# One written order of issue for the whole kernel, with batch 0's attention in two query ranges and the first range as token group 0

## The chip, the cores and the metric

The kernel runs on one core of a Trainium2 chip. Times are device microseconds (us) of that core. "Timed" means the median of plain executions; "span" means the length of the one execution that the profiler recorded, which is 1.7 to 1.9 us shorter than the time of the same execution.

The engines are TensorE (PE in the profile, PEld for its weight loads), VectorE (DVE), ScalarE (ACT), GpSimd (POOL) and SyncE (SP).

## The reference

Squared-ReLU attention, followed by a feed-forward layer with a quick GELU (called the expert layer below).

```python
q, k, v: (8, 12, 448, 64)        # batch, heads, sequence, head_dim
scores = q @ k.T / sqrt(64)
attn   = maximum(scores, 0)**2 / 448
x      = (attn @ v)              # -> 3584 tokens x 768
h      = x @ w_in                # 768 x 2048
g      = h * sigmoid(1.702 * h)
out    = g @ w_out               # 2048 x 768
```

## The kernel before

Attention works on units: 4 of the 12 heads of one batch, so 3 units a batch and 24 in all. Unit u has seven score slots `s u.0` to `s u.6`, one for every 64 keys. A slot is four concurrent 64x64 groups of matmuls, a ReLU from PSUM (on ScalarE, or on VectorE where the slot is marked `d`) and a square on VectorE (`x u.j`). When all seven squares of a unit are there, `a u` multiplies with v and evacuates the result into `xt`, the input of the expert layer.

```python
def relu2(u, j, sc, dve=False):
    ...
    if dve:
        nc.vector.tensor_scalar(out=rl, in0=sc[:, :, 0:S], scalar1=0.0, scalar2=None, op0=ALU.max)
    else:
        nc.scalar.activation(out=rl, in_=sc[:, :, 0:S], func=AF.Relu)
    ...                                   # square now, or when the list says x u.j
```

The expert layer works on groups of tokens, counted in blocks of 64 (`gblk`). First product of step f of group g: six matmuls into `ht`, the gate on ScalarE (`gf`), a scaling on GpSimd (`gt`). The second product of group 0 is plain (32 matmuls for 128 tokens); the later groups use pairs that share sums of weights (56 matmuls for 256 tokens), with a single of 32 where 128 tokens are left over. The sums of weights need all four loaded parts of w_out.

```python
gblk = [6, 8] * (B // 2)                  # 384 and 512 tokens by turns
...
def cast(u, n, eng): ...                  # float32 load -> float16, k on ScalarE, q on GpSimd
def trans(u):   nc.sync.dma_start_transpose(...)       # kT, qT through the DMA
def w2(h, i):   nc.gpsimd.dma_start(out=wout[h][i], in_=...)   # casting load of part i, half h
```

The order of issue is the order in which the program is written; no scheduler moves anything. Up to about 110 us it is a list of words (below, cut). After that a rule mixes first and second products in proportion and puts in a "visit" (three score slots, sometimes an attention product) for every 4.8 us of expert work.

```python
words = ("z3 s0.0 s0.1 x0.0 x0.1 q1 z3 s0.2 ... f14 f15 Q6 K6 R6 x5.5 ... m2 m1 F0 B2 W6 ...").split()
...
for it, tv in moe:                        # the rule, from group 2 on
    ...
    while acc >= tv and visits:
        step_visit()                      # prefetches loads, casts and transposes too
```

## Time and profile before

| | kernel before |
|---|---|
| timed, median of the first 3 runs | 393.91 us (392.98 to 394.2) |
| span of the profiled execution | 391.4 us, granted clock 0.997 |
| first matmul of the expert layer | 31.0 us |
| first matmul of its second group | 64.6 us |
| after the last matmul | 5.4 us |

This is the view of waits of TensorE in the kernel before, from 110 to 330 us; the columns are who waited for whom, us in total, how often, and the longest.

```profile
PE ht L294 <- ACT gf L299: 1.3, 4, 0.3
PE op L361 <- DVE osb L372: 0.5, 1, 0.5
PE op L361 <- ACT ea L370: 0.4, 1, 0.4
PE sc L145 <- ACT rl L159: 0.4, 1, 0.4
```

These named waits add up to 2.6 us. The distances between matmul starts show 7.5 us lost in the same stretch, in the form of small delays that never make the engine idle for long. So the whole document uses one measure, "lost time": the distance from one matmul's start to the next, less its undisturbed distance (columns / 2.4 GHz + 2.5 ns; a quarter of that for each of four concurrent 64x64 matmuls, half for the transposes), less 0.1 us for each change among the three shapes that matmuls have here (the full array, the transposes' 128x64 and the 64x64 tiles; 132 changes before, 135 after).

### The profile page before, as it was taken

How to read it: one execution, taken by the hardware profiler on the slowest of the kernel's cores; microseconds unless marked ns; L12 is line 12 of the kernel's file. 1: busy time of each engine (PE TensorE's matmuls, PEld its weight loads, DVE VectorE, ACT ScalarE, POOL GpSimd, SP SyncE). 2: the span in 40 equal slices, each digit the busy share in tenths (PEclk: the TensorE clock that was granted, in tenths of full speed). 3: DMA queues.
4: the chain of work that ended last, by engine and by line, in shares of the span. 5: the costliest groups of instructions: out<-in, count | busy, mean ns of one | idle time of the engine just before them, and what ended most of it. 6: DMA issues, size and time to landing. Idle time of an engine off the chain costs nothing.

```text
span 391.4 us, 7859 instructions
## 1 busy us (share of the span) xinstructions
PE 375.0 (96%) x3134; PEld 193.6 (49%) x3134; DVE 247.3 (63%) x408; ACT 226.1 (58%) x329; POOL 138.6 (35%) x200
## 2 busy tenths in 40 slices
PE   8779999999999999999999999999999999999993
PEld 3444455445455555444455555444454555554552
DVE  1898965898767675557566767265676767113473
ACT  2887672766676664776675656767675662242210
POOL 8545343634543333242443322341342221232100
PEclk9999999999999999999999999999999999999998
DMA  8999999998956808762474909673234301110323
GB/s 117 195 203 205 204 283 197 197 228 169 197 110 163 203 6 242 145 146 81 77 209 126 226 20 204 122 196 97 52 92 33 82 2 40 42 41 0 83 80 81
DMA packets 65221, 50.85 MB, mean 130 GB/s; under 512 B 35744, under 2 KB 61728, under 8 KB 65184
## 3 DMA queue, kind: packets, MB, share of 16 engines
q1 hardware_dynamic: 47872, 35.70, 36.2%
q0 software_dynamic: 17152, 14.55, 25.4%
q8 instruction: 24, 0.39, 0.4%
q10 hardware_dynamic: 160, 0.10, 0.1%
q14 instruction: 13, 0.11, 0.1%
HBM read 45.61 MB, written 11.01 MB: 145 GB/s over the span
## 4 chain that ended last, share of the span: by engine, by line
PE 78%; DVE 9%; ACT 7%; issue 4%; DMA 1%; POOL 0%; ACTq 0%; POOLq 0%
PE ht L294 32%; PE op L361 26%; PE sc L145 8%; PE av L185 7%; ACT rl L159 4%; PE op L322 4%; DVE osb L372 3%; DVE at L590 3%; ACT k L102 1%; ACT gf L299 1%; DMA q<-in_q_dram 1%; PE tr L129 1%; DVE at L173 1%; PE sc L594 1%; DVE xt L205 0%
## 5 line engine op out<-in xcount | busy, mean ns | idle before, releaser
L159 ACT ACTIVATE rl<-sc 128x896 f16<-128x896 f32 x159 | 140.5, 922 | 39.7 <-PE sc L145 39.4
L294 PE MATMUL ht<-xt,win 128*128 128x384 f16 (+1 forms) x768 | 160.8, 353 | 1.8 <-ACT gf L299 1.3
L301 POOL TENSOR_SCALAR gt<-gf 128x384 f16<-128x384 f32 (+1 forms) x128 | 84.9, 663 | 212.7 <-ACT gf L299 211.6
L299 ACT ACTIVATE gf<-ht 128x384 f32<-128x384 f32 (+1 forms) x128 | 70.1, 548 | 93.9 <-PE ht L294 83.6
L294 PEld LDWEIGHTS <-win 128*128 128x128 f16 x768 | 71.9, 98 | 76.8 <-issue 15.8
L173 DVE TENSOR_TENSOR at<-rl 128x896 f16<-128x896 f16 x105 | 67.8, 672 | 16.4 <-ACT rl L159 16.4
L361 PEld LDWEIGHTS <-gt 128*128 128x128 f16 x408 | 39.0, 98 | 32.1 <-issue 6.0
L145 PE MATMUL sc<-qT,kT 64*64 64x448 f16 x696 | 50.0, 361 | 2.8 <-ACT rl L159 1.8
L590 DVE TENSOR_TENSOR at<-rl 128x896 f16<-128x896 f16 x63 | 41.6, 683 | 8.1 <-ACT rl L159 7.9
L361 PEld LDWEIGHTS <-as 128*128 128x128 f16 x312 | 30.0, 98 | 23.7 <-issue 3.9
L372 DVE SCALAR_TENSOR_TENSOR osb<-op,osb 128x384 f32<-128x384 f32 (+1 forms) x45 | 23.6, 545 | 28.2 <-PE op L361 28.0
L361 PE MATMUL op<-wsum,gt 128*128 128x384 f16 x224 | 40.7, 326 | 0.5 <-ACT ea L370 0.4
L361 PE MATMUL op<-wout,as 128*128 128x384 f16 x224 | 40.7, 326 | 0.3
L205 DVE CAST xt<-av 128x896 f16<-128x896 f32 (+2 forms) x34 | 25.8, 784 | 19.0 <-PE av L185 18.9
L185 PE MATMUL av<-at,v 64*64 64x448 f16 x644 | 34.8, 350 | 0.5 <-ACT rl L159 0.2
L361 PE MATMUL op<-wout,gt 128*128 128x384 f16 (+1 forms) x184 | 32.4, 319 | 1.6 <-DVE osb L372 0.9
L145 PEld LDWEIGHTS <-kT 64*64 64x64 f16 x696 | 17.9, 105 | 29.5 <-issue 20.9
L372 DVE SCALAR_TENSOR_TENSOR osb<-op,ea 128x384 f32<-128x384 f32 x22 | 12.1, 552 | 25.9 <-PE op L361 14.6
L185 PEld LDWEIGHTS <-v 64*64 64x64 f16 x672 | 20.1, 107 | 13.3 <-issue 3.5
L356 DVE TENSOR_TENSOR as<-gt 128x1024 f16<-128x1024 f16 x36 | 26.3, 756 | 0.0
L91 POOL DMA_DIRECT2D v<-in_v_dram x24 | 18.0, 750 | 5.5 <-DMA win<-in_moe_w_in_dram 2.4
L104 POOL CAST q<-qst 128x896 f16<-128x896 f32 x18 | 17.9, 993 | 1.0
(39 smaller groups left out, 178.0 us busy)
## 6 DMA issues: line engine op xcount, KB each, us to landing
out_dram<-osb SPq DMA_DIRECT2D x54, 192.0 KB, 3.1
kst<-in_k_dram SPq DMA_DIRECT2D x18, 448.0 KB, 4.5
qst<-in_q_dram SPq DMA_DIRECT2D x18, 448.0 KB, 5.1
v<-in_v_dram POOLq DMA_DIRECT2D x24, 224.0 KB, 4.4
win<-in_moe_w_in_dram POOLq DMA_DIRECT2D x8, 384.0 KB, 11.5
wout<-in_moe_w_out_dram POOLq DMA_DIRECT2D x4, 768.0 KB, 12.1
k<-in_k_dram POOLq DMA_DIRECT2D x6, 224.0 KB, 9.3
q<-in_q_dram POOLq DMA_DIRECT2D x6, 224.0 KB, 9.3
```

Of the source, the lines that this page charges most:

```text
L145: nc.tensor.matmul(out=sc[c, a, 0:S], lhsT=st["kT"][r, j, c], rhs=st["qT"][r, :, c], start=True, stop=True)
L159: nc.scalar.activation(out=rl, in_=sc[:, :, 0:S], func=AF.Relu)
L173: nc.vector.tensor_tensor(out=at, in0=rl, in1=rl, op=ALU.mult)
L185: nc.tensor.matmul(out=st["av"][s][64 * a:64 * a + 64, 0:S], lhsT=st["v16"][r, a, 64 * j:64 * j + 64], rhs=at[r, a, :], start=(j == 0), st ...
L205: nc.vector.tensor_copy(out=xts[g][:, 2 * pr:2 * pr + 2, c], in_=st["pair"][:, :, f])
L294: nc.tensor.matmul(out=ht[:, 0:n], lhsT=w[:, kk, fo:fo + 128], rhs=xts[g][:, kk, 0:n], start=(kk == 0), stop=(kk == NK - 1))
L299: nc.scalar.activation(out=gf[:, 0:n], in_=ht[:, 0:n], func=AF.Gelu_apprx_sigmoid, scale=1.0 / SC)
L301: nc.gpsimd.tensor_scalar(out=gts[g][:, f, 0:n], in0=gf[:, 0:n], scalar1=SC, scalar2=1.0, op0=ALU.mult, op1=ALU.mult)
L356: nc.vector.tensor_tensor(out=out_, in0=x, in1=y, op=op)
L361: nc.tensor.matmul(out=op[:, 0:cw], lhsT=lhs[:, f, :], rhs=w[:, f, c0:c0 + cw], start=(start and f == 0), stop=(stop and f == HF - 1))
L372: nc.vector.scalar_tensor_tensor(out=o, in0=op[:, 0:w], scalar=sc, in1=add, op0=ALU.mult, op1=ALU.add)
L590: nc.vector.tensor_tensor(out=at, in0=rl, in1=rl, op=ALU.mult)
```

## The change

The intent: start the expert layer earlier, by making its first group out of the first 256 queries of batch 0, and let one optimised list decide every instruction's place instead of the rule. The groups become 4, 8, 8, 8, 6, 8, 6, 8 blocks. The diff, cut to its core:

```diff
-    gblk = [6, 8] * (B // 2)
+    gblk = [4, 8, 8, 8, 6, 8, 6, 8]
...
+    QA = gblk[0]
+    split = slots_of(0, QA) + slots_of(QA, J - QA)     # 4 slots for 256 queries, 3 for 192
+    whole = [[(j, 0, J, 0)] for j in range(J)]
+    def pieces(u):
+        return split if u < NP else whole
...
-        for s in [0, 1] * times:
-            for a in range(2):
+        for kb, q0, q1, c0 in pieces(u)[j] * times:
+            for s in range(2):
+                for a in range(2):
...
+              "a": lambda how, u: av(how, u, 0, J if u >= NP else QA),
+              "b": lambda how, u: av(how, u, QA, J),
...
-        for it, tv in moe:          # the rule, with mix(), visits and prefetch(): all removed
...
+        words = (
+            "z3 jq0 jk0 I jk1 q0 jq2 k0 s0.0:d x0.0 ... s1.6 jk5 x1.5 x1.6 s2.4 jw1 f0.0 ...
+            ... f0.14 s5.0 f0.15 x4.6 Q6 x5.0 ... m0.1.0 a5 m0.0.0 f1.0 jo1.1 jo1.0 f1.1 f1.2
+            Q7 R6 f1.3 s6.0 L8 ... f1.15 s9.0 x8.5 R10 x8.6 L11 a8 W10 s9.1 s9.2 p1.0.0 ...
+            ... p7.2.5 p7.2.6").split()
```

The words: `b u` is the attention product of unit u's second query range, `f g.f` step f of group g's first product, `m`, `p`, `i` are plain, pair and single steps of the second product, `jo h.i` the load of w_out's half h, part i, `A` to `E` its sums, `L`/`W` the loads of q and k / of v, `K` and `Q` the casts, `R` the transposes, `:d` a ReLU on VectorE.

## The prediction

> **What bounds the kernel now.** I read the page's busy shares first, then busy time by stretch, then the chain of work that ended last in two stretches, then VectorE's timeline at the start.
>
> The page's first part (busy time, share of the span, instructions):
>
> ```profile
> PE 375.0 (96%) x3134; PEld 193.6 (49%) x3134; DVE 247.3 (63%) x408; ACT 226.1 (58%) x329; POOL 138.6 (35%) x200
> ```
>
> TensorE (PE) is the only engine near full, so the time is its work plus its gaps. To see where the gaps are, busy time in chosen stretches; columns are the stretch, its length and the busy time and instruction count of PE, weight loads, VectorE, ScalarE and GpSimd, then granted clock, DMA share and rate:
>
> ```profile
> 0.00:31.00 31.00, 24.78 (x341) 12.18 (x341) 20.42 (x39) 19.94 (x24) 19.07 (x32) 1.00 1.11 173
> 31.00:65.00 34.00, 33.39 (x337) 17.23 (x334) 23.86 (x36) 21.13 (x32) 13.57 (x21) 1.00 1.22 227
> 65.00:110.00 45.00, 45.00 (x362) 21.53 (x361) 38.67 (x61) 30.03 (x43) 22.37 (x29) 1.00 1.00 200
> 110.00:330.00 220.00, 216.40 (x1791) 112.35 (x1790) 140.35 (x231) 142.00 (x208) 73.01 (x102) 1.00 0.50 115
> 330.00:386.00 56.00, 55.41 (x314) 30.29 (x312) 23.62 (x44) 12.99 (x23) 10.61 (x17) 1.00 0.19 49
> 386.00:391.40 5.40, 0.01 (x1) 0.00 (x0) 0.36 (x1) 0.00 (x0) 0.00 (x0) 0.75 0.52 139
> ```
>
> Three things: PE loses over 6 us before 31 us, where the first matmul of the expert layer (`ht`) stands; nothing from 65 to 110; 3.6 us from 110 to 330, in bits. The border at 110 is one in the source: up to there the order of issue is a written list, after it a rule spreads the visits. The chain says the same, first for 60 to 110 us, then for 110 to 330 us:
>
> ```profile
> by line: PE ht L294 47.7%; PE op L322 31.0%; PE sc L145 11.3%; PE av L185 7.9%; PE op L361 2.6%
> ```
>
> ```profile
> by line: PE op L361 34.6%; PE ht L294 30.5%; PE av L185 9.1%; PE sc L145 8.7%; ACT rl L159 4.4%; issue 3.7%; DVE osb L372 3.2%; ACT k L102 2.2%; ACT gf L299 1.3%; DVE at L173 1.2%; DVE as L356 0.6%; DVE osb L448 0.3%; ACT eb L370 0.2%; ACT
> ```
>
> In the listed stretch the chain never leaves PE; in the ruled stretch 17% of it runs through ScalarE, VectorE and issue. Busy time hides part of this, since matmuls overlap: I compared the distance between successive matmul starts with their undisturbed distance (162 ns for 384 columns, 215 ns for 512) and find 7.5 us lost from 110 to 330 us, 0.3 us from 60 to 110, 10.7 us before 30 us.
>
> What holds the start? VectorE's timeline (start, length, engine, line, operation, count, idle before):
>
> ```profile
> 10.14 0.62 DVE L590 TENSOR_TENSOR at<-rl 128x896 f16<-128x896 f16 x1 [2.25 <-ACT rl L159]
> ...
> 12.20 0.62 DVE L133 COPY kT<-tr 128x896 f16<-128x896 f16 x1
> ...
> 14.02 2.28 DVE L590 TENSOR_TENSOR at<-rl 128x896 f16<-128x896 f16 x4
> 16.76 1.28 DVE L208 CAST xt<-avm 128x384 f16<-128x384 f32 x4 [0.47 <-PE avm L185]
> ```
>
> From 10 us on VectorE has hardly a gap: squares, copies of transposed tiles, evacuations. It is busy 18 of 20 us between 10 and 30, ScalarE beside it 17.6. So the first 31 us are bound by preparing attention, not by PE.
>
> **What the Trainium skill says.** "Trainium Kernel Development and Optimization", Performance Expectations, calls matmul busy time a bad measure because matmuls are pipelined. The trace agrees: 3.6 us idle against 7.5 us lost. "TensorE: Matmul & The Clock Gate", section "Wait — 56ns, not 53.3ns?", gives N ÷ 2.4 GHz + about 2.5 ns from start to start for a warm array, 215.8 ns for 512 columns; the chain's late row of twelve `ht` matmuls in 2.59 us makes 216, so I trust it for 256 columns (109 ns). The same section puts a floor of about 25 ns under every matmul however short; nothing in this trace is short enough to show it. "TensorEngine Tiling (Array Packing)", Key Properties, says that changing the tiling mode drains the engine: eight `op` matmuls take 1.30 us in the chain after other full ones and 1.41 after attention's 64x64 ones, so about 0.1 us a switch is seen.
>
> **The change part by part.**
>
> *PE's work.* Groups 4,8,8,8,6,8,6,8 put 2 row blocks of 128 in the group that uses the plain second product (32 matmuls a block) where it was 3; 8-groups use pairs (56 for two blocks), 6-groups a pair and a single (88 for three). Before 96 + 3·88 + 4·112 = 808; after 64 + 5·112 + 2·88 = 800. Eight fewer at 0.1625 us is -1.3 us. The six doubled score slots (marked t, pure filler) go: each is four concurrent matmuls, 0.189 us (28 of `av` take 1.32 us), so -1.1 us. Mode switches go from 132 to 135 in the built order: +0.3. First-product columns are unchanged.
>
> *Short matmuls.* Batch 0's three units are cut into 19 pieces where there were 7 slots, for scores and again for `av`, of 64 to 256 columns. The columns are the same. With a floor of 25 ns per matmul a group of four costs at least 100 ns: against 27 ns of columns at 64, 53 at 128, 80 at 192, 107 at 256. The order has 12, 12, 21 and 12 such groups of scores, as many of `av`: at most 2·(12·69 + 12·43 + 21·16) = 3.4 us, an estimate from that page. At least it is some 0.2 us, and part lies in time when PE waits anyway: I take +1.0.
>
> *The start.* The first `ht` no longer waits for all 21 slots of batch 0, but for 12 (its first 256 queries). In VectorE's order 13 squares, 6 copies, a relu and six 128x256 evacuations stand before it: nominally 16 us with the rows' durations (square 0.60 back to back, copy 0.62, relu 1.08, evacuation 0.42 between the 0.21 and 0.55 of 64 and 384 columns), where before it was 22. Before, 22 us were done in 31.1 - 6.2, 89%. The same rate puts the first `ht` at 24.5 us. But that is not yet the gain, as the second group needs all of batches 0 and 1, the same 42 slots as before. Up to its first matmul VectorE has 42·0.60 + 5·1.08 + 12·0.62 + 8.1 (evacuations) + 0.6 = 47 us, before 46. At 89 to 95% it comes to 55.5 to 59 us; PE has 43.5 - 11 = 32.5 us of work between its first `ht` and there, so without a gap 24.5 + 32.5 = 57, which I take; before it was 64.6. By then less PE work is done: 43.5 us counted against 50 (10.5 of first product instead of 15.6, no doubled slots). So the start loses 57 - 43.5 = 13.5 us where it lost 14.6 to 14.7. That is only -1.2. It rests on the 89%; at 95% it is -2.7. Since an optimised list should pack VectorE better, and ScalarE has 39 us of work by then and is not in the way, I take -2.3.
>
> *The rest as a list.* The written stretch from 60 to 110 us lost 0.3 us with VectorE busy 38.67 of 45; the ruled one lost 7.5. If the new list is as good, it saves up to 7. It carries more on VectorE, however: 20 relus there instead of 9 (11·1.08 = 12 us), two more pair sets. Between the middle of group 1's first product and group 2's, VectorE's count is 25 us beside 26 of PE, and in the stretch where one group's second pair stands in a row it is 16 beside 15. I take half to two thirds of the 7.5 as saved: -4.8.
>
> *The end.* The last 14 pair steps are the same in both, so the 5.4 us after the last matmul stay.
>
> Sum on PE's path: 391.4 - 1.3 - 1.1 + 0.3 + 1.0 - 2.3 - 4.8 = 383.2. The median of timed runs is 2.5 over the profiled span (393.9 against 391.4), so 385.7.
>
> **Rivals.** First, VectorE becomes the bound of the middle: for it, the counts just given and 18 us more in total (20 relus); against it, the old listed stretch ran gapless at 86%. Then the rule's 7.5 us stay in another place and the time is 389 to 392. Second, the short matmuls cost their full 3.4 us, and on VectorE's chain: 388. Third, weights come late: the DMA moves some 200 GB/s from 10 to 50 us and is at its limit there; first-group first products want `win` part 1 at about 34 us and part 3 at 45. At 200 GB/s the list's order lands them near 27 and 37 us, so I expect no wait; if one comes, each late part is 2 to 4 us. Fourth, everything pays: the second group at 55 us and 1 us of gaps in the rest makes 381.
>
> **Range and chances.** The terms that I can't fix are the start (-5 to +1), the gaps (-7 to 0) and the short matmuls (+0.2 to +3.4). They are independent, about ±4.5 us together: 381 to 390.5. Two per cent faster is 386.0, within half a microsecond of my number, so faster gets 0.52, same 0.45, slower 0.03.
>
> **What would show it.** Right: first `ht` near 24.5 us, first of the second group at 55 to 59; the chain from 110 to 330 almost all PE; 800 `op` matmuls of 384 columns, counting two of 192 as one; four-matmul groups of 64 columns starting 30 to 100 ns apart. Wrong: PE idle before `op` or `ht` with VectorE named as releaser through the middle; `ht` waiting on a `win` transfer; the second group's start over 60 us; a last stretch other than 5.4 us.

## The result

| | before | after |
|---|---|---|
| timed, median of 4 runs each | 393.98 (392.98 to 394.2) | 389.69 (389.49 to 390.16) |
| span | 391.4 | 388.4 |
| granted clock | 0.997 | 0.999 |

A ratio is the mean time of one kernel's fast runs over that of the other's in the same rounds, so it isn't quite the ratio of the medians. Here it is 0.9898 (95%: 0.9879 to 0.9917): 1.0% faster, within the 2% that counts as the same, where 2.1% faster was predicted. The time lies inside the range of 381 to 390.5, near its upper end.

The page's first part for the kernel after (busy time, share of the span, instructions):

```profile
PE 370.6 (95%) x3390; PEld 195.4 (50%) x3390; DVE 262.4 (68%) x433; ACT 218.4 (56%) x320; POOL 136.8 (35%) x200
```

VectorE has 15 us more, ScalarE 8 us less, mainly because 11 more ReLUs (20 for 9) run on VectorE. TensorE's count grows by the short matmuls. The same stretches as in the prediction, in the same columns (stretch, length, busy time and count of PE, PEld, DVE, ACT, POOL, then clock, DMA share, GB/s; the DMA share is the sum of the packets' times over that of the 16 DMA engines, and as these times overlap it can pass 1):

```profile
0.00:31.00 31.00, 24.16 (x591) 15.90 (x595) 21.27 (x41) 20.87 (x28) 17.82 (x32) 1.00 1.10 172
31.00:65.00 34.00, 32.84 (x400) 18.91 (x393) 24.78 (x43) 22.29 (x36) 16.57 (x26) 1.00 1.12 215
65.00:110.00 45.00, 41.49 (x342) 18.72 (x341) 37.62 (x56) 32.14 (x46) 22.39 (x27) 1.00 1.07 216
110.00:330.00 220.00, 219.40 (x1778) 113.06 (x1776) 156.20 (x254) 130.56 (x191) 69.99 (x101) 1.00 0.53 114
330.00:383.00 53.00, 52.40 (x297) 28.71 (x296) 22.22 (x42) 12.49 (x22) 10.06 (x16) 1.00 0.19 50
383.00:388.40 5.40, 0.33 (x4) 0.10 (x2) 0.36 (x1) 0.00 (x0) 0.00 (x0) 0.93 0.55 147
```

Read the third and the fourth line against those of before. From 110 to 330 us PE's idle time falls from 3.60 to 0.60 us, as hoped. From 65 to 110 us, where the kernel before had none at all (45.00 of 45.00), there are now 3.51 us. The change gives back in one stretch what it gains in another.

The chain of waits from 60 to 110 us of the kernel after: first the shares by line, then the start, length and kind of three of its pieces.

```profile
by line: DMA wout<-in_moe_w_out_dram 27.3%; PE ht L245 18.8%; PE op L271 11.0%; DVE at L453 10.8%; PE sc L166 7.0%; PE op L310 6.6%; DVE rl L177 4.2%; PE av L197 3.7%; ACT gf L250 2.4%; issue 2.3%; DVE xt L217 2.1%; POOL wout L411 1.9%; ACT
...
60.80 0.94 POOL wout L411
...
61.75 13.66 DMA wout<-in_moe_w_out_dram
...
75.45 2.77 PE op L271 x16
```

In the kernel before, this chain was all PE. Here it leaves PE for over half of the stretch. It runs through the load of the second half of w_out, which the list issues at 60.8 and 61.7 us; the kernel before issued its two parts at 44.2 and 53.0 us. The view of waits has PE standing for it once:

```profile
PE op L271 <- DMA wout<-in_moe_w_out_dram: 2.4, 1, 2.4
```

The second place is the row `DVE at`, 10.8% of the chain. The timeline of the kernel after (start, length, engine, line, operation, output and input, count, idle before and its releaser) shows the square that does it, and what PE does afterwards:

```profile
89.02 1.08 DVE L177 TENSOR_SCALAR rl<-sc 128x896 f16<-128x896 f32 x1
...
89.69 0.77 POOL L91 DMA_DIRECT2D v<-in_v_dram  x1
...
90.02 1.88 DVE L453 TENSOR_TENSOR at<-rl 128x896 f16<-128x896 f16 x1
...
90.47 0.94 POOL L104 CAST q<-qst 128x896 f16<-128x896 f32 x1
...
95.97 1.45 PE L197 MATMUL av<-at,v 64*64 64x448 f16 x24 [0.52 <-DVE rl L177]
97.99 0.38 PE L197 MATMUL av<-at,v 64*64 64x448 f16 x4 [0.57 <-DVE at L453]
```

A square of this shape takes 0.62 us; this one takes 1.88, beside GpSimd's issue of the load of v and its cast of q for unit 10. It ends 0.49 us after the cast does. VectorE's queue is 1.3 us late from then on, and PE pays in the next attention product, 5 us later: lost time of 1.45 us at 95 to 98 us. The same thing happens at 130.87 us beside unit 13's cast (2.10 us). The kernel before has such a square too (1.86 us at 75.25 us, beside a cast at 75.68), and PE loses nothing after it, so a slow square alone doesn't make a loss. What differs may be how soon PE needs what VectorE has queued behind it; no run tests that by itself.

The third view is the chain from 110 to 330 us of the kernel after:

```profile
by line: PE ht L245 40.5%; PE op L310 35.1%; PE sc L166 9.7%; PE av L197 8.3%; DVE at L453 2.4%; DVE osb L321 1.3%; issue 1.1%; DVE rl L177 0.5%; ACT rl L180 0.4%; DVE gt L305 0.3%; DVE as L305 0.3%; ACT eb L319 0.2%; ACT ea L319 0.2%; ACTq
```

PE's own four rows are 93.6% of it, where they were 82.9% before. Lost time over all stretches, in us:

| | 0-30 | 30-60 | 60-110 | 110-330 | 330-end | span |
|---|---|---|---|---|---|---|
| before | 11.83 | 1.57 | 0.36 | 7.50 | 1.16 | 391.4 |
| after | 10.84 | 2.46 | 4.63 | 2.58 | 1.17 | 388.4 |
| after, second profile (below) | 11.55 | 2.64 | 3.11 | 2.60 | 1.17 | 387.7 |

The rest of the difference is work: full-array matmuls -1.30 us, 64x64 matmuls -0.96, three more switches +0.3, the tail -0.3. With the lost time's -0.74 this makes the 3.0 us between the two spans.

So three questions go to the chip. Is w_out late only because it is issued late (order), or because the DMA can't bring it sooner without taking from others (supply)? Is the loss at 95 to 98 us due to GpSimd's cast, or to the ReLUs moved to VectorE? And what are the split start and the list worth each by itself?

### The profile page after: what moved, and what is told of

Its sections match the earlier page's. It is cut to its first block, busy times and chain, and to the rows that moved or that the text cites. A ratio compares the mean times of both kernels' runs of the same rounds, so it can differ in the third digit from the quotient of the medians.

```text
span 388.4 us, 8391 instructions
## 1 busy us (share of the span) xinstructions
PE 370.6 (95%) x3390; PEld 195.4 (50%) x3390; DVE 262.4 (68%) x433; ACT 218.4 (56%) x320; POOL 136.8 (35%) x200
## 4 chain that ended last, share of the span: by engine, by line
PE 79%; DVE 9%; DMA 6%; issue 3%; POOL 2%; ACT 1%; ACTq 0%; POOLq 0%
PE ht L245 34%; PE op L310 27%; PE sc L166 8%; PE av L197 6%; DVE at L453 4%; DMA wout<-in_moe_w_out_dram 4%; DMA v<-in_v_dram 2%; PE op L271 2%; DVE osb L321 2%; DVE rl L177 1%; PE tr L129 1%; PE avm L197 1%; DVE xt L220 1%; ACT rl L180 1%; POOL k L119 1%
## 5 line engine op out<-in xcount | busy, mean ns | idle before, releaser
L245 PE MATMUL ht<-xt,win 128*128 128x512 f16 (+2 forms) x768 | 157.9, 353 | 0.2 <-ACT ea L319 0.2
L252 POOL TENSOR_SCALAR gt<-gf 128x512 f16<-128x512 f32 (+2 forms) x128 | 82.6, 645 | 214.0 <-ACT gf L250 212.4
L180 ACT ACTIVATE rl<-sc 128x896 f16<-128x896 f32 x148 | 130.1, 922 | 45.3 <-PE sc L166 37.0
L250 ACT ACTIVATE gf<-ht 128x512 f32<-128x512 f32 (+2 forms) x128 | 69.7, 548 | 87.8 <-PE ht L245 75.2
L166 PE MATMUL sc<-qT,kT 64*64 64x448 f16 (+4 forms) x816 | 48.2, 324 | 2.3 <-ACT rl L180 1.5
L217 DVE CAST xt<-av 128x768 f16<-128x768 f32 (+5 forms) x34 | 24.1, 735 | 20.4 <-PE av L197 20.4
L321 DVE SCALAR_TENSOR_TENSOR osb<-op,osb 128x384 f32<-128x384 f32 (+1 forms) x49 | 25.7, 545 | 15.4 <-PE op L310 15.2
L310 PE MATMUL op<-wout,gt 128*128 128x384 f16 (+1 forms) x200 | 35.3, 320 | 0.8 <-DVE osb L321 0.8
L197 PE MATMUL av<-at,v 64*64 64x448 f16 (+3 forms) x668 | 33.1, 331 | 1.2 <-DVE at L453 0.6
L177 DVE TENSOR_SCALAR rl<-sc 128x896 f16<-128x896 f32 x20 | 21.7, 1086 | 6.5 <-PE sc L166 6.4
```

The costliest lines, as they stand in the source:

```text
L166: nc.tensor.matmul(out=sc[c, a, c0:c0 + 64 * (q1 - q0)], lhsT=st["kT"][r, kb, c], rhs=st["qT"][r, q0:q1, c], start=True, stop=True)
L197: nc.tensor.matmul(out=st["av"][s][64 * a:64 * a + 64, 64 * (q0 - base):64 * (q1 - base)], lhsT=st["v16"][r, a, 64 * kb:64 * kb + 64], rhs ...
L217: nc.vector.tensor_copy(out=xts[g][:, 2 * pr:2 * pr + 2, c], in_=st["pair"][:, :, f])
L245: nc.tensor.matmul(out=ht[:, 0:n], lhsT=w[:, kk, fo:fo + 128], rhs=xts[g][:, kk, 0:n], start=(kk == 0), stop=(kk == NK - 1))
L250: nc.scalar.activation(out=gf[:, 0:n], in_=ht[:, 0:n], func=AF.Gelu_apprx_sigmoid, scale=1.0 / SC)
L252: nc.gpsimd.tensor_scalar(out=gts[g][:, f, 0:n], in0=gf[:, 0:n], scalar1=SC, scalar2=1.0, op0=ALU.mult, op1=ALU.mult)
```

## The experiments

Sixteen kernels ran, in four calls of four; each call shares its runs of the kernel before. Its medians were 392.39, 392.99, 392.96 and 393.41 us, so across calls the ratios are compared, not the medians (the record names three chips, and the fourth call's list of the kernel before is the third's with one run added). "Lost" is the count above.

### Move the load of w_out: earlier, later, and a little earlier

```diff
 # e1_wout_early, in the list
-  ... f0.11 x4.3 f0.12 ... s5.0 f0.15 x4.6 Q6 ... m0.0.0 f1.0 jo1.1 jo1.0 f1.1
+  ... f0.11 jo1.1 x4.3 f0.12 ... s5.0 f0.15 jo1.0 x4.6 Q6 ... m0.0.0 f1.0 f1.1
```

> The changed kernel with its last two weight loads (second half of w_out) issued at the places they had in the old list, some 18 and 12 us earlier. Theory A, these loads come too late: the 2.4 us wait of op for wout at 72.6 us and most of the 1.5 us of gaps at 95 to 98 us go, which followed from VectorE standing behind its weight sums; 385.5 to 387.0 us. Theory B, VectorE is too full there because of relus put on it: the loss between 60 and 110 us (4.3 us over before) stays or moves to waits for VectorE; 388.8 to 390 us.

Measured: 392.44 us (391.51 to 394.33), ratio 0.9992 (0.9948 to 1.0035). That is over both forecasts. The wait for w_out is gone and yet the kernel is slower than the one after. The chain of waits of e1_wout_early, from 36 to 135 us (start, length, kind):

```profile
48.18 9.61 DMA qst<-in_q_dram
57.84 0.94 POOL q L104
58.80 8.82 DMA qT<-q
67.75 0.76 PE sc L166 x12
```

The load of unit 6's q now takes 9.61 us and its transposition 8.82, beside the early w_out, where the kernel after has 6.73 and 2.94; PE waits 3.3 us for `qT` instead. An earlier issue alone is therefore no remedy: in this profile the DMA share is above 1.0 from 10 to 80 us, and what is given to one transfer comes later for another. The gaps after the slow square stay, now at 97 and 99 us.

```diff
 # e2_wout_later
-  ... m0.0.0 f1.0 jo1.1 jo1.0 f1.1 f1.2 Q7 R6 f1.3 s6.0
+  ... m0.0.0 f1.0 f1.1 f1.2 Q7 R6 f1.3 jo1.1 jo1.0 s6.0
```

> The opposite dose: the same two loads issued three first-product steps later than in the changed kernel, about 4 us. Theory A: the wait for wout grows one for one, 392.5 to 395 us. Theory B: no more than 1 us, up to 390.7 us.

Measured: 398.26 us (396.81 to 398.96), ratio 1.0129 (1.0089 to 1.0169). PE's wait for w_out in this run:

```profile
PE op L271 <- DMA wout<-in_moe_w_out_dram: 8.9, 1, 8.9
```

Lost time from 60 to 110 us rises to 12.68. So the load is on PE's path, and moving it later is paid in full and more: issued 5.0 us later, it lands 7.2 us later. About 1.6 us of the loss is the clock's: from 75.8 to 86.0 us the granted clock is 0.50, and the sixteen `op` matmuls at the end of the wait take 4.40 us where they take 2.77 in the kernel after.

```diff
 # e7_wout_after_q6
-  ... f0.15 x4.6 Q6 x5.0 ... m0.0.0 f1.0 jo1.1 jo1.0 f1.1
+  ... f0.15 x4.6 Q6 jo1.1 jo1.0 x5.0 ... m0.0.0 f1.0 f1.1
```

> The two loads of the second half of w_out issued right after the cast of unit 6's q, between the places of the changed kernel and of the first trial: some 5 us earlier, but behind the loads of units 6 and 7 on which the first trial stood. Theory E with a slot free there: wout lands at 69 to 70 us, the wait for it goes and none for q comes, 386.5 to 388 us. If no slot is free: 388.5 to 391 us with a new wait of PE for a transposed tile of unit 6 to 8.

Measured: 388.87 us (388.24 to 391.32), ratio 0.9914 (0.9876 to 0.9952), beside 0.9915 of the unaltered kernel. The wait is gone, the span is 386.9 against 387.7, lost time from 60 to 110 us is 2.16 against 3.11; the gaps at 93.6 and 95.6 us stay. In this profile the load behind unit 6's q makes nobody else wait (e9 and e11 below, with the load in the same place, do show a wait), but the runs scatter by 3 us and no gain in time is shown.

### The kernel after again, and the kernel without that load

The second kernel of this pair gives a wrong result on purpose (relative error 0.76): the second half of w_out isn't loaded but filled by VectorE at the start.

```diff
 # e5_after_again: no edit
 # e6_no_wout1_load
-  ... f1.0 jo1.1 jo1.0 f1.1
+  ... f1.0 f1.1
+  nc.vector.memset(wout[1][0], 0.01)
+  nc.vector.memset(wout[1][1], 0.01)
```

> The changed kernel unaltered, as the yardstick on this chip: about 0.990 of before, 389 to 390.5 us, with the wait of op for wout (2.4 us at 73 us) and the gaps at 95 to 98 us in place again.

> Wrong result on purpose: the second half of w_out is not loaded but set to a constant by VectorE while it has nothing to do at the start, 1.6 MB as float16 or some 8 us at 200 GB/s. Theory E, the transfers up to 75 us are at their limit and any late load only moves the wait: with the load gone neither wout nor a q transpose is waited for, the gaps between 60 and 110 us fall by 2.4 to 4 us, 385.5 to 387.5 us. Rival F, the order of VectorE and ScalarE bounds the stretch: within 1 us of the changed kernel.

Measured: 389.53 us (389.29 to 389.92), ratio 0.9915 (0.990 to 0.993) for the kernel after; 388.29 (387.71 to 389.92), ratio 0.9889 (0.9865 to 0.9914) without the load. In its second profile the kernel after loses 1.07 us at this place, not 2.4. The view of waits puts it down to ScalarE's gate (`gf`, 0.9 us), which ended last, but the load landed at 74.76 us, 0.05 us before PE went on, and without the load PE goes on at 73.6 us although that gate ends at 74.7. So it is the same wait, and it varies from one execution to another. Theory E expected 2.4 to 4 us less loss and got 1.1. Without the load 2.03 us are lost from 60 to 110 us, and 1.45 of them are the two gaps after the slow square. That is what e5 shows there (3.11) less its wait (1.07), so the load explains its own wait and nothing of the rest.

### The ReLUs on VectorE

```diff
 # e3_no_dve_relu: all 20 ":d" marks removed
-  s0.0:d ... s3.2:d ... s22.5:d
+  s0.0 ... s3.2 ... s22.5
```

> All 20 relus that the new list gives to VectorE go to ScalarE, order unchanged. Theory B: the gaps between 60 and 110 us shrink by 2 us or more, 386 to 388 us. Theory A: VectorE's load isn't the cause, the wait for wout stays at 2 us or more, and ScalarE's added 17 us (20 times 0.85) land partly on the path: 389.5 to 393 us.

Measured: 391.54 us (390.83 to 391.97), ratio 0.9961 (0.9926 to 0.9996), span 389.4. PE now waits 3.4 us for ScalarE's ReLUs; lost time rises from 2.5 or 2.6 to 3.4 us between 30 and 60 and from 2.6 to 3.8 between 110 and 330, and from 60 to 110 it is 3.0. So taking the ReLUs off VectorE is no gain; without them the span is 1.7 us longer than that of e5_after_again. Yet they may have a part in the second loss. With no ReLU in front of it on VectorE, the square that was slow is over before the cast begins (0.62 us from 90.15, the cast from 90.85), and the two gaps at 95 to 98 us are gone. Waits for ScalarE stand in their place.

### GpSimd's cast beside VectorE's square

```diff
 # e8_q10_scalar
-  "Q": lambda how, u: cast(u, "q", nc.gpsimd),
+  "Q": lambda how, u: cast(u, "q", nc.scalar if u == 10 else nc.gpsimd),
```

> One cast, q of unit 10, on ScalarE instead of GpSimd. A square of 0.6 us beside it took 1.88 us on VectorE. Theory G, VectorE and GpSimd get in each other's way in this place and that makes the 1.5 us of gaps at 95 to 98 us: they shrink by 0.7 us or more, 388 to 389 us on the scale of the changed kernel's 389.7. Rival: VectorE is merely full there; no change or up to 1 us more, as ScalarE carries another 0.95 us.

Measured: 387.78 us (387.07 to 389.1), ratio 0.9874 (0.9851 to 0.9896) beside 0.9915 of the unaltered kernel, span 385.5. The timeline of e8_q10_scalar at the same place:

```profile
88.36 0.77 POOL L91 DMA_DIRECT2D v<-in_v_dram  x1
...
88.69 0.61 DVE L453 TENSOR_TENSOR at<-rl 128x896 f16<-128x896 f16 x1
...
90.73 0.97 ACT L102 ACTIVATE q<-qst 128x896 f16<-128x896 f32 x1
```

The same square now takes 0.61 us, with the load of v still issued beside it, and the gaps at 95 to 98 us are gone. So the second loss comes from the meeting of square and cast, shown by taking the one cast away with all ReLUs in place. (In e3 the meeting doesn't come about either.) "SBUF — State Buffer", section "Who interferes with whom", says that a VectorE instruction with two inputs in SBUF contends with a GpSimd instruction that reads SBUF. The same section has it that the shared ports are an exclusive lock and that the order of issue decides which of the two blocks.

The traces agree in most meetings, and not with casts alone: GpSimd's gate scalings (`gt`) hold squares as well. In the profile of the kernel after, twenty squares began inside a cast or a scaling and were held; they took 0.68 to 1.35 us and ended 0.47 to 0.48 us after that instruction. Where a square's record begins first, it mostly takes its 0.62 us and GpSimd's instruction is the longer one: the cast beside the square of 54.11 us took 1.29 us, where 0.94 is usual. Two squares don't fit, and they are the slowest: those of 90.02 and 130.87 us stand 0.45 and 0.67 us ahead of their casts, and lost. Both began while GpSimd was issuing a load of v with the cast next in its queue. Whether the cast takes hold before its record begins stays open.

### The parts together

```diff
 # e9_both          = e7_wout_after_q6 + e8_q10_scalar
 # e11_both_q13     = e9_both, and
-  nc.scalar if u == 10 else nc.gpsimd
+  nc.scalar if u in (10, 13) else nc.gpsimd
 # e13_casts_only   = the kernel after, with this line alone (w_out's load not moved)
```

> The two repairs together: second half of w_out issued after the cast of unit 6's q, and unit 10's q cast on ScalarE. If the wait for wout (1.0 to 2.4 us) and the gaps at 95 to 98 us (1.5 us) are separate, they add up: 386.0 to 387.5 us, ratio to before 0.982 to 0.986; loss between 60 and 110 us under 1 us. If one hides the other: 387.5 us or more.

> Both repairs and unit 13's q cast on ScalarE too, since a square beside a GpSimd cast at 131 us took 2.1 us and PE had gaps of 0.85 us at 133 and 137 us. If those come from the same meeting: 0.4 to 0.9 us under the run with both repairs. Rival: the gap at 137 us is an evacuation's turn and ScalarE's cast costs as much as it saves; no difference beyond 0.3 us.

> The changed kernel with the q casts of units 10 and 13 on ScalarE and the loads where they were: 386.5 to 388 us, ratio 0.983 to 0.987; of the loss between 60 and 110 us only the wait for wout of 1 to 2.5 us is left. If it is as fast as the run with the weights moved as well (0.9853), moving the weights is worth nothing.

Measured: e9 388.05 us (387.04 to 390.87), ratio 0.9881 (0.9852 to 0.9911); e11 387.0 (386.46 to 389.31), ratio 0.9853 (0.9828 to 0.9878); e13 387.54 (387.26 to 388.39), ratio 0.9865 (0.9841 to 0.9888). The two remedies don't add: with both of them PE waits 0.9 us for a `qT` (0.8 in e11) that it didn't wait for before, so moving the load once more exchanges one wait for another. The cast of unit 13 is worth 0.77 us of lost time from 110 to 330 us (2.58 to 1.81). e11 and e13 can't be told apart by time. In e13 the loss at the wait for w_out is 0.76 us, under the 1 to 2.5 expected. Both give the right result and beat both kernels: e13 is one line away from the kernel after.

### What is left of the loads

```diff
 # e15_no_load_casts = e13_casts_only + e6_no_wout1_load (wrong on purpose, relative error 0.76)
```

> Wrong result on purpose: the casts on ScalarE, and the second half of w_out not loaded at all but set by VectorE at the start. Both theories: no wait for wout, loss between 60 and 110 us under 0.8 us, 1 to 2.5 us under the casts alone; it is what a perfect order of transfers could reach.

Measured: 385.94 us (385.33 to 386.06), ratio 0.9814 (0.9795 to 0.9833). Lost time from 60 to 110 us is 0.56, against 1.32 in e13. The chain of e15_no_load_casts from 60 to 110 us:

```profile
by line: PE ht L245 59.1%; PE sc L166 14.0%; PE op L271 10.6%; PE av L197 8.4%; PE op L310 8.2%
```

It is all PE again, as in the kernel before. The load of w_out, with what it takes from other transfers, and the meeting on the port are thus nearly the whole of what the new list loses there beyond the old one's 0.36.

```diff
 # e14_l8_later = e13_casts_only, unit 8's loads and what hangs on them later
-  f1.3 s6.0 L8 C1 ... s6.1:d K8 R7 C3 ... x6.1 Q8 W6 x6.0 L9 R8 ... f1.5 A0 ... f1.7 f1.8 x6.2 W7
+  f1.3 s6.0 C1 ... s6.1:d R7 L8 C3 ... x6.1 W6 x6.0 L9 ... f1.5 K8 A0 ... f1.7 Q8 f1.8 x6.2 W7 R8
```

> As before it, and the loads of unit 8's k and q with their casts and transposes some 8 us later, which leaves the transfers to the weights. Order theory: the wait for wout falls under 0.5 us with no new one, 1 to 2 us under the casts alone. Supply theory: the wait returns as one for a transfer of unit 7 or 8 and the time is within 0.7 us of the casts alone, or over.

Measured: 396.44 us (395.21 to 397.07), ratio 1.008 (1.0059 to 1.0101). This is a miss of the experiment. The timeline and then the view of waits of e14_l8_later:

```profile
77.10 0.95 ACT L102 ACTIVATE k<-kst 128x896 f16<-128x896 f32 x1 [9.23 <-DMA kst<-in_k_dram]
```

```profile
PE ht L245 <- ACT gf L250: 8.2, 1, 8.2
```

ScalarE works in program order, so it stood 9.2 us at the cast whose load my edit had put too late, and the gates behind it stood as well. (The granted clock is 0.50 from 74.6 to 81.4 us of this profile, which adds over 1 us.) It shows how dear a load in the wrong place is, but not whether some order of these transfers would have served all of them.

### The start and the list, each by itself

```diff
 # e4_old_start: batch 0 whole again, the old list's words up to the sixth f, the new ones after
-        return split if u < NP else whole
+        return whole
-        base = QA if u < NP and j >= QA else 0
+        base = 0
-  z3 jq0 jk0 I jk1 q0 jq2 k0 s0.0:d x0.0 ... f0.5 b2 f0.6
+  jk0 jq0 I k0 q0 ... z3 s0.0 s0.1 x0.0 x0.1 q1 z3 s0.2 ... f0.5 f0.6
 # e10_old_start_both  = e4_old_start + e9_both
 # e16_old_start_casts = e4_old_start + e13_casts_only
```

> New groups and new list, but batch 0 not split: up to the sixth step of the first product the old list's order, whole slots, no doubled scores. Theory C, the split moves the first product forward without gaining time, as both starts are bound by VectorE: 389 to 391 us, second group's first product within 1.5 us of 58 us. Rival D, the split is where the 4 us come from: 392 us or more.

> The same two repairs on the kernel with batch 0 whole and the old start. If the split gains 2 us in the first 60 us, which the wait for wout then took back, it now shows: 1.5 to 3 us over the run with both repairs. If the split is worth nothing even so: within 0.7 us of it.

> The casts on ScalarE, batch 0 whole, old start. If the split is worth 2 us: 1.5 to 3 us over the casts alone, with the first 60 us losing about 15.7 us where it is 13.5. If it is worth nothing: within 0.7 us.

This edit takes the old order of the first loads along with the whole slots, so what is measured is the split together with its order of start. Measured, with time, ratio and lost time before 60 us beside that of the split kernel with the same remedies:

| | time | ratio | lost before 60 | split, lost before 60 |
|---|---|---|---|---|
| e4 | 391.17 (390.09 to 391.69) | 0.9958 | 15.67 | 13.30, 14.19 |
| e10 | 393.39 (390.94 to 396.06) | 1.001 | 15.85 | 13.71 |
| e16 | 391.16 (389.54 to 392.93) | 0.9953 | 17.60 | 14.54 |

With the same small first group, the split start saves 1.5 to 2.4 us before 60 us in the first two rows. The third shows 3.1, but e16's profile has the clock at half from 21.9 to 25.3 us and loses 1.66 us there, where e10 loses 0.14 in the same piece of work; without that it is about 1.5, an estimate from these numbers. In time e10 lies 5.3 us above e9 and e16 3.6 above e13, more than the 1.5 to 3 expected. Part of that is the clock as well: e10's six runs go from 390.94 us at a mean granted clock of 0.999 to 396.06 at 0.985. e4 lies between its two forecasts, with its second group at 60.4 us instead of 56.5 to 59.5; it loses only 2.46 us from 60 to 110, as it arrives later at w_out. But the kernel before, with its larger first group, loses 13.40 us by then, no more than the split one: its 384 tokens give PE 15.6 us of first product in a stretch where the others are the bound, instead of 10.5. That is an argument; no run changes the size of the group alone.

```diff
 # e12_rule_rest: the new groups, start and list up to x8.6; from there the old rule, written out
-  ... x8.6 L11 a8 W10 s9.1 s9.2 p1.0.0 x9.0 D1 E2 f2.0 x9.2 p1.0.1 s9.3:h E0 Q11 ...
+  ... x8.6 (remaining weight sums and loads) L11 s9.0 a8 s9.1 s9.2:h f2.0 x9.0 f2.1 x9.1 p1.0.0 f2.2 ...
```

> The changed kernel's groups, split start and list up to the last square of unit 8 (about 98 us), and from there the old rule of the kernel before instead of the list. If the list is what took 4.9 us of gaps out of the stretch from 110 to 330 us: 393.5 to 396 us on the scale of the changed kernel's 389.6, with 7 us lost there. If the new grouping alone did it: 389 to 391 us.

Measured: 397.07 us (395.79 to 397.23), ratio 1.0089 (1.0063 to 1.0115), over its forecast. The window from 110 to 330 us of e12_rule_rest, in the columns of above:

```profile
110.00:330.00 220.00, 217.12 (x1764) 110.87 (x1763) 144.14 (x236) 141.46 (x205) 69.93 (x98) 1.00 0.51 116
```

PE is idle for 2.88 us there instead of 0.60, and lost time is 6.58 instead of 2.58 us: 4.0 us from the list alone. The rest of this kernel's loss lies at the seam, where the sums put there hold up VectorE (7.22 us lost from 60 to 110, one stall of 2.58 us at 98 us among them, and 1.6 us at half clock from 102.1 to 105.5 us); that part is my edit's and not the rule's.

## Why the prediction was right and wrong

**The work of TensorE: right.** Eight fewer matmuls were put at -1.3 and measured -1.30 us; three more switches (135) came as counted.

**The short matmuls: mis-sized.** They were put at +1.0 us with a floor of 25 ns each. Groups of four concurrent 64-column matmuls start 28 ns apart, those of 128, 192 and 256 columns 56, 83 and 109 ns: the columns alone, and for 64 columns just under the 30 to 100 ns named as the mark. The 64x64 work fell by 0.96 us, which is the -1.13 of the doubled slots and +0.17 of the short ones. The second rival (3.4 us) is dead by the same number. (The differences to 100 ns that the prediction lists, 73, 47 and 20 ns, would have made 3.7 us; its sum has 69, 43 and 16.)

**The start: right in its marks, wrong in its term.** The first `ht` was to come near 24.5 us. The durations listed for it add up to 15.1 us and not to 16, which at the same 89% makes 23.2. In the timeline of the kernel after it comes sooner still:

```profile
22.50 0.83 PE L245 MATMUL ht<-xt,win 128*128 128x256 f16 x6
```

The second group came at 57.9 us, within the 55 to 59. By the prediction's own count (57 - 43.5 = 13.5 lost, where it was 14.6 to 14.7) this makes 14.4 us, so about -0.3. Lost time before 60 us says the same. The step that failed is "Since an optimised list should pack VectorE better ... I take -2.3", which added 1.1 us beyond the count. In its place the runs show no gain: 13.40 us lost before, 13.30 and 14.19 after. What the count did say, that an earlier first `ht` is no gain by itself, held: 8.5 us earlier gave next to nothing.

**The rest as a list: right from 110 us on, wrong before.** -4.8 was expected out of the 7.5; from 110 to 330 us lost time went down by 4.9, and e12 shows 4.0 for the list alone. The step that failed is that the term spoke of the ruled stretch only. "The written stretch from 60 to 110 us lost 0.3 us" was used as proof of what a list can do, though the change rewrites that stretch as well and could only lose there. It lost 4.3 us more (2.8 in the second profile): 2.4 or 1.1 waiting for w_out, 1.45 after one square held up by a cast (e8). Some 0.6 to 0.8 remained after these. e15 takes both causes away and comes to 0.56.

**The rivals.** The first named VectorE as the bound of the middle; e3 speaks against it, as the loss from 60 to 110 us is no smaller without the ReLUs (3.04, beside 3.11 in e5). It was near the truth in one respect: VectorE's queue was what PE waited for at 95 to 98 us, through a meeting with GpSimd's cast that doesn't come about in e3. The third, late weights, was right in kind ("each late part is 2 to 4 us") and wrong in name: it looked at `win` in the first group, and it was `wout` in the second one's time. Its premise, that the DMA is at its limit to 50 us, reaches further: the stretch from 65 to 110 us still has a DMA share of 1.07 (1.00 in the kernel before).

**The sum.** Predicted span 383.2, measured 388.4: a miss of 5.2. The terms give it: start 2.2 (-0.1 for -2.3), rest 4.1 (-4.92 + 4.27 = -0.65 for -4.8, with rounding), short matmuls -0.8, tail -0.3. In time the miss is 4.0, since the 2.5 us added for the difference between span and median were 1.3 in this kernel.

**What stays open.** The wait for w_out differs from one execution to another (2.4 and 1.07 us), and so does the place of the stretches at half clock. Whether an order of the transfers before 75 us exists that makes nobody wait wasn't found: e1, e9 and e14 each moved the wait elsewhere, and e7 removed it for 0.8 us of span, with no gain in time shown. e15, which leaves this load out, shows what there is to win at this place: 385.94 against 387.54 us, 1.6.

## What to carry to other kernels

When a change rewrites more than the stretch that it is meant for, give each rewritten stretch its own term, and for a stretch without gaps that term can only be a loss. Look in it for the next shared thing, here the DMA and the port between VectorE and GpSimd, before reading anything from how well the old order did there. A slow instruction off the path is paid for by the matmul unit several us later, so compare each instruction's length with that of its own kind before looking at who waited.

## What the Trainium skill lacked or had wrong

- "TensorE: Matmul & The Clock Gate", section "Wait — 56ns, not 53.3ns?": the floor of about 25 ns from start to start is given without exception, and the prediction took it to hold for concurrent matmuls too. The same page's section "Measured speedup vs the span model" has about 4 ns per tile instead. The trace agrees with that one: concurrent 64x64 matmuls start 3 to 4 ns apart, and a group of four with 64 columns takes 28 ns to the next group's start.
- "TensorEngine Tiling (Array Packing)", Key Properties: it names the drain on a change of mode and gives no cost. Here the start after a full-array matmul of 384 columns comes after 256 ns instead of 162 when the next one uses 64x64 tiles, and the start after a 448-column group's last matmul after 282 ns instead of 179 when the next one uses the full array: about 0.1 us each way.
- "SBUF — State Buffer", section "Who interferes with whom": the block of a two-input VectorE instruction by a GpSimd instruction that reads SBUF is seen (squares of 1.88 and 2.10 us for 0.62), and so is the rule of order in most meetings. These two squares' records, however, begin 0.45 and 0.67 us before the casts' and they lost all the same. The section speaks of the order of issue and the trace shows starts, so this doesn't prove it wrong; it doesn't say how long before its recorded start an instruction can hold the ports.
